# ScalarE issues the stores of what it wrote itself; a first cast and an expert step change their places

## The chip, the cores and the metric

The kernel runs on one core of one Trainium2 chip. Its engines are called PE (TensorE: matmuls, and the loads of their stationary operand as PEld), DVE (VectorE), ACT (ScalarE), POOL (GpSimd) and SP (SyncE, which only issues DMAs here). The metric is the device time of one launch in microseconds (us). The kernel before was run three times: 2190.37 us is the median, from 2181.95 to 2191.92.

## What is computed

The input x has 8 batches of 5696 tokens by 128 channels. Each channel is convolved with a filter h as long as the sequence, and the result goes through a mixture of 8 experts of which each token takes one:

```python
Xf = np.fft.rfft(x, n=2 * S, axis=1)
Hf = np.fft.rfft(h, n=2 * S, axis=0)
y = np.fft.irfft(Xf * Hf[None], n=2 * S, axis=1)[:, :S, :]
...
logits = x @ w_gate                      # x is now y, 45568 x 128
expert_idx = np.argmax(logits, axis=1)
...
for e in range(E):                       # 8 experts
    mask = expert_idx == e
    h = np.maximum(x[mask] @ w1[e], 0.0) # 128 -> 1024
    ye = h @ w2[e]                       # 1024 -> 128
    out[mask] = gate_w[mask, None] * ye
```

## The kernel before

The Fourier transform is split in two steps, both done as matmuls, with the data in device memory between them. The batches form three groups of 2, 3 and 3. Every group goes through three stages:

- **A, forward transform** (`steps_a`). An item is one batch and four of the 48 residues. Its tile xt is loaded (L277), cast to the matmul's type on ACT (L268, tile xc, first half), and the rest that the cast lost is subtracted on POOL or DVE (L269, second half). Both halves go through PE (L290) twice, once for the real part (c = 0) and once for the imaginary part (c = 1). `store` copies the result to the tile ut, the real part on ACT, the imaginary part on DVE (L302). When the last batch of the group is in ut, its store to U is put on the list `late`, and `flush` (L283) issues all on the list from SP, a step later. `start` loads the first items and casts the first one; `begin` loads one item ahead, casts the next one and issues the matmuls.
- **B, products** (`phase_b`). For four frequencies at a time, uq is loaded from U, transformed further (L503 to L509), multiplied with the filter's spectrum hh (L535 to L550), and transformed back (L562, L566). For group 0, `filt` and `filt_save` make the spectrum from h on the way, and a store puts it into HS for the other groups. For groups 1 and 2, ACT copies each result to vt (L587). HS and V (tile vt) also go through a list `late`, which SP works off once per step of the loop (L628).
- **C, inverse and routing** (`phase_c`). vq is loaded from V, cast (L705) and split (L706), transformed (L742), turned, scored against the gate, routed to an expert, ranked among that expert's tokens, and scattered by POOL into SR, which is ordered by expert. The ranks of a part come from counts of earlier tiles: `score` makes two small matmuls with a matrix of ones and a triangular one (L785, L786) on the choices of the tile before, into the tile gb. The last tile's counts are made by `score(None, n - 2)` when nothing is left to score; they need the choices oh of the last tile, which a chain on DVE makes.

Beside B and C of groups 1 and 2 the expert layers run (`experts`): xr is loaded from SR, turned to xtb, multiplied with w1 (L1098, tile mh), the relu is split between ACT (L1104) and DVE (L1108), multiplied with w2 (L1120, tile ma), and written out by POOL (L1143). A step is a quarter of a tile: six matmuls of each layer. The weights wb are loaded by SP from WD (L1067) under a condition, so most of these 728 issues move nothing. C of group g (g = 0, 1) has A of the next group beside it: for group 1 as an ordinary stream (`phase_a`), for group 2 as a **guest** inside C of group 1 (`Guest`, whose `begin` and `end` are called in the loop of `phase_c`). `rest` calls `guest.start()` twelve steps before B of group 1 ends, so that the loads are on their way.

The order is written by hand: all functions are generators, and `run` takes from the stream that has the lowest sum of stated costs so far. What comes out is one fixed list of instructions per engine, and each engine works its list in order. So an instruction that waits holds everything behind it on its engine. `yield STEP` in `phase_c` states a cost without issuing anything, which lets an expert step come first.

DMAs that SP and ACT issue share eight completion counters, taken in turn in the program's order. The DMA that takes a counter waits until the one that had it before, eight places earlier, has landed. Before the change ACT issues only the nine loads of constants (L199) in stage A of group 0; SP issues all other hardware DMAs. POOL has its own queue for the scatters and for one table.

Of the kernel before, what the change touches and what calls it, by code (L numbers as in the profile page):

```python
# [23 lines left out]
NB = 48  # L24
# [35 lines left out]
STEP = 1065  # L60
# [5 lines left out]
def conv_moe(ctx: ExitStack, tc: tile.TileContext, I, out, B, S, D, E, F, split):  # L66
    nc = tc.nc
# [70 lines left out]
    for g, nbs in enumerate(split):  # L138
        gr = Group(g, b0, sum(nbs))
# [9 lines left out]
    HS = dram.tile([NB, QN, 2, D], F32, name="HS")  # L149
# [3 lines left out]
    state = {"rests": False, "hold": 0, "space": False, "spare": None}  # L153
# [97 lines left out]
    def steps_a(gr, tag, bufs):  # L251
        g, nb = gr.g, gr.nb
        srcs = [(I["x"][gr.b0 + b], b) for b in range(nb)]
        tw = 4 * D
        items = []
        for ig in range(NB // 4):
            for src, b in srcs:
                items.append((ig, src, b))
        xts, uts, xss = {}, {}, {}
        fore = 2 if g > 1 else 4  # L260
        split = A3[g]

        def cut(n):
            if not split or n >= len(items):
                return
            xt = xts.pop(n)
            xs = sb.tile([MP, 2, tw], F32R, tag="us", name=f"xc{g}_{n}", bufs=3 if g > 1 else 2)
            nc.scalar.copy(xs[:, 0], xt)  # L268
            getattr(nc, ALO[g]).tensor_tensor(out=xs[:, 1], in0=xt, in1=xs[:, 0].bitcast(F32), op=ALU.subtract)  # L269
            xss[n] = xs  # L270

        def load(n):
            if n >= len(items):
                return
            ig, src, b = items[n]
            xts[n] = sb.tile([MP, tw], F32, tag="xt", name=f"xt{g}_{n}", bufs=1 + fore)
            nc.sync.dma_start(xts[n], src[:, ig * tw : (ig + 1) * tw])  # L277

        banks, late = {}, []

        def flush():
            while late:
                nc.sync.dma_start(*late.pop(0))  # L283

        def transform(m):
            n, c = divmod(m, 2)
            banks[m] = ps.tile([P, 512], F32, tag="cx", name=f"pa{g}_{n}_{c}", bufs=4)
            ops = [(fcs[:, c], xts[n])] if not split else [(fcr[:, u, c], xss[n][:, v]) for u, v in PASSES]
            for k, (lhs, rhs) in enumerate(ops):
                nc.tensor.matmul(banks[m][:QN, :], lhs, rhs, start=(k == 0), stop=(k == len(ops) - 1))  # L290
            if c == 1:
                (xss if split else xts).pop(n)

        def store(m):
            n, c = divmod(m, 2)
            ig, src, b = items[n]
            if b == 0:
                uts[c] = sb.tile([QN, 4, gr.cols], F32, tag=tag, name=f"ut{g}_{ig}_{c}", bufs=bufs)
            srcv = banks.pop(m)[:QN, :].rearrange("p (i d) -> p i d", d=D)
            lo = c * NB + ig * 4  # L300
            cp = nc.scalar.copy if c == 0 else nc.vector.tensor_copy
            cp(uts[c][:, :, b * D : (b + 1) * D], srcv)  # L302
            if b == nb - 1:
                late.append((gr.U[:, lo : lo + 4, :], uts[c]))

        def start():
            for n in range(fore):
                load(n)
            cut(0)

        def begin(m):
            if m % 2 == 0:
                load(m // 2 + fore)
                cut(m // 2 + 1)
            transform(m)

        return start, begin, store, flush, 2 * len(items)
# [107 lines left out]
    def phase_b(gr):  # L425
        g, cb, cw, nch, QB, PK = gr.g, gr.cb, gr.cw, gr.nch, gr.qb, gr.pk
        iw = PK * cw
        lags = BLAGS[PK - 1]
        tiles, outs_ = {}, {}
# [36 lines left out]

        mats, hhs, hbank, cuts, whole = {}, {}, {}, {}, {}
        cutting = F3[g]
        state, banks, late = {}, {}, []

        def filt(qb, k0):
            if g != 0 or qb * QB >= QN:
# [6 lines left out]
        def filt_save(qb, m):  # L479
            if qb not in hbank:  # L480
                return
            hp = hbank[qb]
            if m == 0:
                hhs[qb] = hhbufs[qb % 3]
            hh = hhs[qb]
            c2, k = divmod(m, 2)
            nc.scalar.mul(hh[k * HP : (k + 1) * HP, :, c2, :], hp[c2 * HP : (c2 + 1) * HP], -1.0 if m == 3 else 1.0)
            if m == 3:
                hbank.pop(qb)
                late.append((HS[:, qb * QB : qb * QB + QB], hh[:NB, :QB]))  # L490

        def forward(n):
            q, c = items[n]
# [81 lines left out]
        def save(n):  # L575
            q, c = items[n]
            qb, k0 = divmod(q, QB)
            if g == 0:
                nc.scalar.copy(
                    wide[:, q : q + PK], banks.pop(n)[:, : PK * cb * K2].rearrange("p (q b x) -> p q b x", b=cb, x=K2)  # L580
                )
                if k0 + PK == QB:
                    tiles.pop(qb), hhs.pop(qb), mats.pop(qb)
                return
            if k0 == 0 and c == 0:
                outs_[qb] = sb.tile([K2, QB, gr.cols], F32, tag="six", name=f"vt{g}_{q}", bufs=SIX)
            nc.scalar.copy(  # L587
                outs_[qb][:, k0 : k0 + PK, c * cw : (c + 1) * cw],
                banks.pop(n)[:K2, :iw].rearrange("p (q x) -> p q x", q=PK),
            )  # L590
            if k0 + PK == QB and c == nch - 1:
                late.append((gr.V[qb * QB : qb * QB + QB].rearrange("q p c -> p q c"), outs_.pop(qb)))
                tiles.pop(qb), hhs.pop(qb), mats.pop(qb)

        items = [(q, c) for q in range(0, QN, PK) for c in range(nch)]
# [17 lines left out]
        for n in range(N + lags[3] + 2):  # L613
            qb, at = divmod(n, per)
            for k0 in range(at * PK, (at + 1) * PK):
                if k0 == 1:
                    load_m(qb + (3 if g == 0 else 2))
                if k0 == min(3, per * PK - 1):
                    load(qb + 2)
                if k0 == 0:  # L620
                    filt(qb + 1, QB - 1)
                    if qb:
                        filt_save(qb, 3)
                else:
                    filt(qb + 2, k0 - 1)
                    filt_save(qb + 1, k0 - 1)
            while late:
                nc.sync.dma_start(*late.pop(0))  # L628
            if n < N:
                forward(n)  # L630
                if n % per == per - 1:
                    load_whole(qb + 2)
            cut(n + CUT)
            dp, dc, di, ds_ = lags
            if 0 <= n - di < N:
                inverse(n - di)
            if 0 <= n - dp < N:
                product(n - dp)
            if 0 <= n - dc < N:
                combine(n - dc)  # L640
            if 0 <= n - ds_ < N:
                save(n - ds_)
            yield PK * max(cw * 7 / 2.4 + 200, 2 * cw / 0.96 + 300) if g == 0 else RATE[3 * g - 2] * iw * 8 / 2.4
# [28 lines left out]
    def phase_c(pt, guest=None):  # L672
        gr, g, nb, cb, cw, NI, ns = pt.gr, pt.s, pt.nb, pt.cb, pt.cw, pt.ni, pt.ns
# [204 lines left out]
        for n in range(n_end + 1):  # L878
            for k in range(nsub):
                at = n * nsub + k  # L880
                if k == (1 if n == 0 else 0):
                    load(n + 2)
                if n < nu:
                    synth(n, k)
                if TL <= at < total_sub + TL:
                    tp = ps.tile([P, 512], F32, tag=ytag, name=f"tp{g}_{n}_{k}", bufs=ybuf)
                    turn(*divmod(at - TL, nsub), tp)
                if k == nsub - 1 and n >= 1:
                    score(n - 1, n - 2 if g else None)
                if k == 0 and n >= (n_end if g else 2):  # L890
                    score(None, n - 2)
                lift(at + 2)
                if guest:
                    guest.begin(1 if k == nsub - 1 and n >= 1 else 2)
                yield cost if n < nu else cost / 2
                if guest:
                    guest.end()
                if n < nu:
                    divide(*divmod(at + AHEAD, nsub))
                    settle(n, k)  # L900
                lifted(at + 2)
                if 0 <= at - TL < total_sub:
                    turned(*divmod(at - TL, nsub))
                chains = []
                if g and k == nsub - 1 and 0 <= n - 2 < nu:
                    chains.append(rank(n - 2))
                if k == nsub - 1 and 0 <= n - 1 < nu:
                    chains.append(route(n - 1))
                if k == 0 and n >= (n_end if g else 2):
                    chains.append(rank(n - 2))  # L910
                zipped(*chains)
                if n == n_end:
                    break
# [515 lines left out]
```

## Time and profile before

| | us |
|---|---|
| median of three runs (lowest, highest) | 2190.37 (2181.95, 2191.92) |
| profiled execution | 2188.59 |
| its span, first to last instruction | 2186.7 |
| mean granted clock of PE, share of full speed | 0.974 |
| stage A of group 0 with the filter's transform | 0 to 81 |
| B of group 0 | 81 to 230 |
| C of group 0 with A of group 1 | 230 to 407 |
| B of group 1, then C of group 1 with the guest | 407 to 720, 720 to 960 |
| B of group 2, then C of group 2 | 960 to 1401, 1401 to 1650 |
| a last stretch of filling and sorting, then experts alone | 1650 to 1700, 1700 to 2187 |

The stages' borders are read from the trace and rounded. In a row of a timeline stand the start, the busy time, the engine, the line, the operation with the tiles it writes and reads, the shape, and in brackets the idle time ahead of it on its engine with what released it. In a row of waits stand the waiting line, what it waited for, the sum, the number of waits and the longest. The granted clock is the share of full speed that the power throttle allowed PE.

The 40 slices of the span give the course of things (busy tenths of each engine; the clock that PE was granted; the share of time that the 16 DMA engines were busy):

```profile
PE   9999899799999999988999999999998999999998
PEld 7889676467676888987888888999998999999998
DVE  5688576799898677768888878666666555555554
ACT  6677555234343566644555545565554444444444
POOL 7466265535454277777878777456664344443333
PEclk9999999699999999999999999999999999999999
DMA  8899798899897798977788787466552443343331
```

### The profile page before, as it was taken

What the parts mean: (1) busy time and instruction counts of PE and PEld (TensorE: products, weight loads), DVE (VectorE), ACT (ScalarE), POOL (GpSimd) and SP (SyncE); (2) the same over time, 40 slices, a digit from 0 to 9 for tenths busy, and PEclk for the clock granted to TensorE, in tenths of its full rate; (3) what the DMA queues carried; (4) which work ended last, traced back from release to release, by engine and by line L of the source; (5) the groups of instructions that cost most, each with busy time, mean ns of one, the idle gap of its engine ahead of it and who ended that gap; (6) DMA issues with size and microseconds to landing.
All of it is one profiled execution on the core that took longest, in us unless ns stands there. A gap on an engine that the chain in (4) does not pass through costs nothing. (4 is left out here: it accounts for less than half of the span.)

```text
span 2186.7 us, 46733 instructions
## 1 busy us (share of the span) xinstructions
PE 2091.7 (96%) x14458; PEld 1864.4 (85%) x14458; DVE 1538.1 (70%) x3365; ACT 1118.7 (51%) x2323; POOL 1236.6 (57%) x1215
## 2 busy tenths in 40 slices
PE   9999899799999999988999999999998999999998
PEld 7889676467676888987888888999998999999998
DVE  5688576799898677768888878666666555555554
ACT  6677555234343566644555545565554444444444
POOL 7466265535454277777878777456664344443333
PEclk9999999699999999999999999999999999999999
DMA  8899798899897798977788787466552443343331
GB/s 279 245 278 292 219 276 262 247 230 260 229 256 182 215 278 255 269 197 210 199 223 225 190 210 197 137 163 170 125 139 80 141 129 106 128 130 125 121 119 34
DMA packets 218366, 424.80 MB, mean 194 GB/s; under 512 B 32661, under 2 KB 136587, under 8 KB 218116
## 3 DMA queue, kind: packets, MB, share of 16 engines
q1 hardware_dynamic: 189711, 365.62, 60.6%
q0 software_dynamic: 27296, 55.94, 8.8%
q8 instruction: 117, 1.92, 0.4%
q14 instruction: 133, 1.09, 0.2%
q10 hardware_dynamic: 1109, 0.23, 0.1%
HBM read 582.74 MB, written 154.27 MB: 337 GB/s over the span
## 5 line engine op out<-in xcount | busy, mean ns | idle before, releaser
L1108 DVE SCALAR_TENSOR_TENSOR hs<-mh,hs 128x512 fp32r<-128x512 f32 x728 | 501.7, 689 | 394.7 <-ACT hs L1104 388.1
L1098 PE MATMUL mh<-xtb,wb 128*128 128x256 f32 x4368 | 703.5, 297 | 22.9 <-DMA wb<-WD 17.8
L1104 ACT ACTIVATE hs<-mh 128x512 fp32r<-128x512 f32 x728 | 435.8, 599 | 482.2 <-PE mh L1098 478.2
L1120 PE MATMUL ma<-hs,wb 128*128 128x256 f32 x4368 | 659.3, 287 | 11.1 <-DMA wb<-WD 11.1
L1098 PEld LDWEIGHTS mh<-xtb,wb 128*128 128x128 f32 x4368 | 590.8, 191 | 92.8 <-issue 38.6
L1120 PEld LDWEIGHTS ma<-hs,wb 128*128 128x128 f32 x4368 | 574.6, 191 | 14.1 <-DMA wb<-WD 13.7
L1143 POOL DMA_INDIRECT out<-xr x314 | 311.6, 992 | 438.5 <-DVE xr L1134 372.6
L655 POOL DMA_INDIRECT SR<-rt,pi x384 | 408.4, 1064 | 242.2 <-issue 74.9
L550 POOL TENSOR_TENSOR zt<-zt,xs 128x384 f32<-128x384 f32 (+1 forms) x280 | 297.2, 1070 | 138.7 <-DVE xs L540 84.4
L587 ACT COPY vt<-vp 96x384 f32<-96x384 f32 x240 | 114.3, 476 | 270.3 <-PE vp L566 268.5
L544 DVE TENSOR_TENSOR xs<-xp,hh 64x384 f32<-64x384 f32 (+1 forms) x360 | 214.8, 597 | 7.8
L535 DVE TENSOR_TENSOR zt<-xp,hh 128x384 f32<-128x384 f32 (+1 forms) x300 | 173.6, 579 | 40.6 <-PE xp L509 27.4
L566 PE MATMUL vp<-zt,mi 128*96 128x384 f32 x480 | 201.4, 501 | 0.3 <-issue 0.3
L509 PE MATMUL xp<-uq,mt 96*128 96x256 f32 (+1 forms) x480 | 172.1, 464 | 9.6 <-ACT vt L587 5.6
L290 PE MATMUL pa<-xc,fcr 120*120 120x512 f32 x576 | 163.8, 417 | 7.2 <-ACT hh L727 5.4
L540 DVE SCALAR_TENSOR_TENSOR xs<-xp,hh 64x384 f32<-64x384 f32 x240 | 134.3, 560 | 4.2
L290 PEld LDWEIGHTS pa<-xc,fcr 120*120 120x120 f32 x576 | 99.5, 187 | 34.3 <-ACT hh L727 8.0
L742 PE MATMUL yp<-vr,gcr 120*120 120x384 f32 x576 | 119.2, 342 | 7.3 <-ACT ut L302 5.8
L566 PEld LDWEIGHTS vp<-zt,mi 128*96 128x96 f32 x480 | 79.3, 167 | 49.9 <-issue 27.6
L509 PEld LDWEIGHTS xp<-uq,mt 96*128 96x128 f32 x480 | 86.1, 203 | 34.8 <-ACT vt L587 13.0
L706 DVE TENSOR_TENSOR vr<-vq,vr 120x768 fp32r<-120x768 f32 x96 | 91.5, 954 | 30.8 <-ACT vr L705 30.2
L742 PEld LDWEIGHTS yp<-vr,gcr 120*120 120x120 f32 x576 | 97.4, 185 | 10.5 <-ACT ut L302 8.1
(160 smaller groups left out, 2572.1 us busy)
## 6 DMA issues: line engine op xcount, KB each, us to landing
wb<-WD SPq DMA_DIRECT2D x728, 512.0 KB
U<-ut SPq DMA_DIRECT2D x48, 720.0 KB
uq<-U SPq DMA_DIRECT2D x60, 576.0 KB
V<-vt SPq DMA_DIRECT2D x60, 576.0 KB
vq<-V SPq DMA_DIRECT2D x48, 720.0 KB
xt<-x SPq DMA_DIRECT2D x96, 240.0 KB
hh<-HS SPq DMA_DIRECT2D x120, 192.0 KB
xr<-SR SPq DMA_DIRECT2D x157, 130.0 KB
```

Of the source, the lines that this page charges most:

```text
L290: nc.tensor.matmul(banks[m][:QN, :], lhs, rhs, start=(k == 0), stop=(k == len(ops) - 1))
L509: nc.tensor.matmul(to, mt[:, k0 + s, :], uc, start=True, stop=True)
L544: nc.vector.tensor_tensor(out=xs[to], in0=x3[at], in1=him, op=ALU.mult)
L550: eng.tensor_tensor(out=zt, in0=zt, in1=xs, op=ALU.add)
L566: nc.tensor.matmul(vp[:K2, s * cw : (s + 1) * cw], mi[:, k0 + s, :], zt[:, s].rearrange("p b d -> p (b d)"), start=True, stop=True,)
L655: s = nc.gpsimd.indirect_dma_start(out=SR[:, :], out_offset=IndirectOffsetOnAxis(ap=pi[:, b : b + 1], axis=0), in_=rt[:, b, :], in_offset= ...
L742: nc.tensor.matmul(yp[:MP, :cw], lhs, rhs, start=(m == 0), stop=(m == len(ops) - 1))
L1098: nc.tensor.matmul(hp[:, u, :], wb[:, a, f, :], xt[:, b, :], start=(n == 0), stop=(n == 2))
L1104: done = nc.scalar.activation(hs[:, 0], hp, AF.Relu)
L1108: nc.vector.scalar_tensor_tensor(out=hs[:, 1], in0=hp, scalar=0.0, in1=hs[:, 0].bitcast(F32), op0=ALU.max, op1=ALU.subtract)
L1120: nc.tensor.matmul(accs[j], wb[:, a, f, :], hs[:, b, u, :], start=(k == 0 and u == 0 and n == 0), stop=(k == NPAIR - 1 and u == 1 and n == 2),
L1143: sc = nc.gpsimd.indirect_dma_start(out=out[:, :], out_offset=IndirectOffsetOnAxis(ap=xr[:, s, D + 1 : D + 2].bitcast(I32), axis=0), in_=x ...
```

## The change

Three things are edited.

1. **Stores.** The store of U's real half, of HS and of V is issued by ACT (`nc.scalar.dma_start`), right behind ACT's own copy, in place of the list that SP works off. U's imaginary half, which DVE writes, stays on the list and on SP. These are 36 + 30 + 60 = 126 issues, and the loop over the list in `phase_b` goes.
2. **First cast.** `cut(0)` moves from `start` to `begin(0)`. For `phase_a` the two follow each other, and nothing moves. For the guest, `start` comes during B of group 1 and `begin(0)` in C of group 1.
3. **Counts.** Ahead of the last `score(None, n - 2)` of parts 1 and 2 stands a `yield STEP`.

```diff
@@ store, in steps_a
             if b == nb - 1:
-                late.append((gr.U[:, lo : lo + 4, :], uts[c]))
+                if c == 0:
+                    nc.scalar.dma_start(gr.U[:, lo : lo + 4, :], uts[c])
+                else:
+                    late.append((gr.U[:, lo : lo + 4, :], uts[c]))
 
         def start():
             for n in range(fore):
                 load(n)
-            cut(0)
 
         def begin(m):
+            if m == 0:
+                cut(0)
             if m % 2 == 0:
@@ phase_b
-        state, banks, late = {}, {}, []
+        state, banks = {}, {}
...
-                late.append((HS[:, qb * QB : qb * QB + QB], hh[:NB, :QB]))
+                nc.scalar.dma_start(HS[:, qb * QB : qb * QB + QB], hh[:NB, :QB])
...
-                late.append((gr.V[qb * QB : qb * QB + QB].rearrange("q p c -> p q c"), outs_.pop(qb)))
+                nc.scalar.dma_start(gr.V[qb * QB : qb * QB + QB].rearrange("q p c -> p q c"), outs_.pop(qb))
...
-            while late:
-                nc.sync.dma_start(*late.pop(0))
             if n < N:
@@ phase_c
                 if k == 0 and n >= (n_end if g else 2):
+                    if g:
+                        yield STEP
                     score(None, n - 2)
```

The following rows are the instructions of one engine in their order, with the line, the operation, and the tiles written and read; the numbers at the end of a name tell buffers apart and differ between the two kernels. Lines of the changed kernel lie up to four further down. First ACT during B of group 1, before the change, where the guest's first cast (xc_0) stands between copies to vt, which PE's next results need out of their way:

```order
L1088 CAST xtb_7941<-mx_16_7900 128x256
L587 COPY vt_100_7925<-vp_102_0_7929 96x384
L1104 ACTIVATE hs_3_7981<-mh_3_7951 128x512
L587 COPY vt_100_7925<-vp_103_0_7972 96x384
L268 CAST xc_0_8025<-xt_0_8021 120x512
L587 COPY vt_104_8041<-vp_104_0_8012 96x384
L1104 ACTIVATE hs_0_8043<-mh_0_7997 128x512
```

Then ACT in the changed kernel at the beginning of C of group 1, where it stands now:

```order
L1108 ACTIVATE hs_0_8645<-mh_0_8632 128x512
L707 CAST vr_0_0_8663<-vq_0_8528 120x768
L707 CAST vr_0_1_8666<-vq_0_8528 120x768
L268 CAST xc_0_8676<-xt_0_8022 120x512
L268 CAST xc_1_8681<-xt_1_8024 120x512
L1108 ACTIVATE hs_1_8692<-mh_1_8648 128x512
```

The cast went from between two groups of four copies to behind the casts of vr, right ahead of item 1's cast; DVE's subtraction L269 went with it.

Next SP at the end of B of group 1, before the change: the last store of V among the loads of weights (each has an ISA row that reads its condition).

```order
L1067 ISA
L1067 DMA wb_0_0_4784<-WD 128x1024
L1067 ISA
L1067 DMA wb_0_3_4790<-WD 128x1024
L628 DMA V_73<-vt_116_8406 96x4x384
L1067 ISA
L1067 DMA wb_0_1_4786<-WD 128x1024
```

And ACT in the changed kernel, with the same store:

```order
L1134 COPY ot_8447<-ma_8294 128x256
L591 COPY vt_116_8403<-vp_118_0_8421 96x384
L591 COPY vt_116_8403<-vp_119_0_8468 96x384
L596 DMA V_73<-vt_116_8403 96x4x384
L1108 ACTIVATE hs_2_8473<-mh_2_8449 128x512
L1092 CAST xtb_8476<-mx_19_8456 128x256
```

The store left SP's row and stands on ACT directly behind the copy that completes vt, ahead of a relu.

Last PE at the end of C of group 2, where the last counts (gb_None) are made, before the change:

```order
L791 MATMUL gb_23_22_24349<-c_moe_w_gate,yt_23_24292 120x8 x6
L785 LDWEIGHTS ones
L785 MATMUL gb_None_24382<-oh_23_24376,ones 128x54
L786 LDWEIGHTS lt
L786 MATMUL gb_None_24382<-oh_23_24376,lt 120x54
L1098 MATMUL mh_0_24403<-xtb_24328,wb_0_0_13345 128x256 x6
L1120 MATMUL ma_24284<-hs_2_24322,wb_0_3_13518 128x256 x6
```

And in the changed kernel:

```order
L793 MATMUL gb_23_22_24349<-c_moe_w_gate,yt_23_24292 120x8 x6
L1102 MATMUL mh_0_24400<-xtb_24328,wb_0_0_13345 128x256 x6
L1124 MATMUL ma_24284<-hs_2_24322,wb_0_3_13518 128x256 x6
L787 LDWEIGHTS ones
L787 MATMUL gb_None_24413<-oh_23_24376,ones 128x54
L788 LDWEIGHTS lt
L788 MATMUL gb_None_24413<-oh_23_24376,lt 120x54
```

One expert step (mh, ma) went ahead of the two count matmuls; at the end of C of group 1 the same happens.

## The prediction

> **What bounds the kernel now.** I read the page's table of engines first, then the table by stage, then the waits of PE, and last the waits of the queues. The first line gives busy time, share of the span and number of instructions of each engine.
>
> ```profile
> PE 2091.7 (96%) x14458; PEld 1864.4 (85%) x14458; DVE 1538.1 (70%) x3365; ACT 1118.7 (51%) x2323; POOL 1236.6 (57%) x1215
> ```
>
> PE is the bound: of the span of 2186.7 us only 95.0 us (2186.7 less 2091.7) are idle on PE. A change that takes no matmul away can win only from these 95 us and from stretches at a lower granted clock. ACT, which gets the new work, is idle for half of the span. The table by stage gives for each stretch its length, the busy time of PE, PEld, DVE, ACT and POOL, the granted clock, the DMA share and GB/s.
>
> ```profile
> 81.00:230.00 149.00, 138.97 (x955) 129.57 (x956) 124.58 (x183) 104.33 (x195) 95.38 (x76) 0.97 0.99 270
> 230.00:407.00 177.00, 161.55 (x861) 120.58 (x859) 112.90 (x338) 90.42 (x201) 90.82 (x85) 0.97 0.85 252
> 407.00:720.00 313.00, 297.55 (x1475) 209.95 (x1476) 274.90 (x529) 110.24 (x236) 153.11 (x155) 0.91 0.90 232
> ```
>
> The rows are the products of the first group, its inverse with the next group's forward transform beside it, and the products of the second group. They hold 41 of the 95 us (10.0 + 15.5 + 15.5), at a DMA share of 0.85 to 0.99. The experts alone, which come last, hold none of the edits and stay. PE's waits (us in total, times, longest) over the whole span:
>
> ```profile
> PE mh L1098 <- DMA wb<-WD: 17.8, 11, 3.3
> PE ma L1120 <- DMA wb<-WD: 11.1, 8, 3.2
> PE gb_None L785 <- DVE sm L826: 7.9, 11, 1.6
> PE yp L742 <- ACT ut L302: 5.8, 5, 1.9
> PE xp L509 <- ACT vt L587: 5.6, 7, 2.2
> PE pa L290 <- ACT hh L727: 5.4, 6, 1.3
> PE xp L509 <- DMA uq<-U: 4.0, 2, 3.1
> ...
> PE ph L390 <- ACT uc L405: 1.6, 2, 0.9
> ```
>
> Nothing here is one big wait. Loads of weights (17.8 and 11.1) are the largest, and all go through SP's queue. That queue waits in order; its own rows are:
>
> ```profile
> SPq L283 <- ACT ut L302: 65.7, 26, 7.7
> ...
> SPq L628 <- ACT vt L587: 28.4, 21, 5.5
> ...
> SPq L443 <- DMA uq<-U: 20.6, 12, 2.6
> ...
> SPq L628 <- ACT hh L487: 10.5, 13, 3.8
> ```
>
> So SP stands 104.6 us (65.7 + 28.4 + 10.5) ahead of stores whose data ACT has not written yet, with later loads behind them. These three waits go. What remains of SP's limits is in the third row: it waits for landings, because each DMA takes one of eight counters in turn and can't issue before the DMA eight places earlier has landed.
>
> **The guest's first cast.** The ACT row (start, length, in brackets the idle time before it and its releaser), PE's row, and the table of stretches around them:
>
> ```profile
> 681.38 0.62 ACT L268 CAST xc<-xt 120x512 fp32r<-120x512 f32 x1 [6.05 <-DMA xt<-x]
> ```
>
> ```profile
> 682.43 1.65 PE L509 MATMUL xp<-uq,mt 96*128 96x384 f32 x2 [2.17 <-ACT vt L587]
> ```
>
> ```profile
> 640.00:680.20 40.20, 39.77 (x218) 29.31 (x215) 34.26 (x64) 14.14 (x30) 21.84 (x23) 1.00 1.01 267
> 680.20:682.40 2.20, 0.06 (x1) 0.00 (x0) 0.37 (x1) 1.02 (x3) 0.00 (x0) 0.98 1.01 306
> 682.40:689.10 6.70, 6.67 (x21) 4.91 (x22) 6.53 (x12) 2.07 (x5) 2.00 (x2) 0.50 0.90 225
> ```
>
> ACT waits 6.05 us for a load that nobody needs for another 50 us; the V copies behind it are late, PE stands for 2.17 us, and then the granted clock is 0.50 for 6.7 us. In that stretch PE did 21 matmuls in 6.70 us, 3.13 per us, where ahead of the gap it did 218 in 40.20, 5.42 per us. So it did 3.9 us worth of work (6.70 x 3.13 / 5.42) and lost 2.8. Together 2.17 + 2.8 = 5.0 us, an estimate, since the matmuls differ in size; if only half of 6.7 is lost it is 5.5. What is late next? DVE, with 6.53 of 6.70 busy: but it is catching up there after the same stall, and ahead of it ran at 34.26 of 40.20. The cast's new place is here, in ACT, DVE and PE rows:
>
> ```profile
> 730.67 0.62 ACT L268 CAST xc<-xt 120x512 fp32r<-120x512 f32 x1
> ```
>
> ```profile
> 731.81 0.69 DVE L269 TENSOR_TENSOR xc<-xt,xc 120x512 fp32r<-120x512 f32 x1
> ```
>
> ```profile
> 732.99 1.56 PE L290 MATMUL pa<-xc,fcr 120*120 120x512 f32 x6
> ```
>
> These are item 1's cast, its subtraction, and item 0's matmul. With the change item 0's cast takes the slot at 730.67 and its subtraction ends at 732.50, still ahead of 732.99; item 1 comes 0.6 to 0.7 us later and has until its own matmuls. The cost lies between 0 and 1.3 us (0.62 + 0.69); I take 0, because PE is at that time in the inverse's matmuls. **-5.0.**
>
> **Stores on ACT: what SP gains.** Of one place all rows are seen: SP's row of V and of the weights behind it, then PE's wait, then the clock.
>
> ```profile
> 716.43 0.32 SPq L628 DMA_DIRECT2D V<-vt  x1
> 717.11 1.83 SPq L1067 DMA_DIRECT2D wb<-WD  x2
> ```
>
> ```profile
> 722.90 1.29 PE L1098 MATMUL mh<-xtb,wb 128*128 128x256 f32 x6 [1.88 <-DMA wb<-WD]
> ```
>
> ```profile
> 723.30:726.70 3.40, 3.40 (x18) 3.40 (x17) 1.38 (x3) 0.97 (x2) 0.18 (x1) 0.50 1.03 275
> ```
>
> Without the store the weights could issue up to 0.68 us earlier (717.11 less 716.43), more only if their own buffer were free before. The bounds are 0 and 3.6 (the wait of 1.88 and half of 3.40 at half clock); I take 1.5, since one part of the clock's loss may go with the shorter gap. All other places together, among them one where a store of V stands ahead of weights and the rest where no store does, I put at 0.5; the bound above is the sum of the load rows, in the first rival. In the first transform the last real halves of U stand in SP behind loads for the next stage, and PE's row of L390 shows what that costs: 1.6 us, so 0 to 1.6, and I take 0.8. The imaginary halves stay on SP and hold it at the same places as now. **-2.8.**
>
> **Stores on ACT: what ACT pays.** 126 issues move: 36 of U, 30 of HS, 60 of V. No store has ever been issued on ACT here; the nearest rows are those on SP (min/median/max ns).
>
> ```profile
> L283 SPq DMA_DIRECT2D U<-ut x72: 316/328/2895, 10.7 to 951.8; - x72
> ```
>
> ```profile
> L628 SPq DMA_DIRECT2D V<-vt x60: 317/334/1459, 436.5 to 1394.2; - x60
> L628 SPq DMA_DIRECT2D HS<-hh x30: 308/376/1105, 84.4 to 220.6; - x30
> ```
>
> By the medians that is 36 x 0.328 + 30 x 0.376 + 60 x 0.334 = 43.1 us more on an engine that is idle for 1068 us. Each store also waits for the copy right ahead of it on ACT, so it hides behind nothing on ACT itself; it is hidden where ACT's next instruction waits for PE anyway. For V (60) and U of the last group (12) that holds, since the relu behind them is what waits for PE:
>
> ```profile
> ACT hs L1104 <- PE mh L1098: 478.2, 566, 5.0
> ```
>
> I take 0, between 0 and 2. In the stages without experts cover is thin. The first is the spectrum's store in the first group's products:
>
> ```profile
> 103.93 0.59 ACT L487 ACTIVATE hh<-hp 64x512 f32<-64x512 f32 x1 [0.59 <-ACT hh L487]
> ```
>
> ACT has a pause of 0.59 us, the shorter kind, where the store now stands, and 0.376 fits. If each issue took the row's maximum of 1.1, 0.5 would stick out, 15 us over 30 stores; I take the median and +1. In the first transform 12 stores are 3.9 us, with ACT waiting for PE between (+1, from 0 to 4). In the first inverse 12 more are 3.9 us, and there PE already waits for ACT's copies (L727 5.4, in the list above), so half shows: +2, from 0 to 4. **+4, between 0 and 25.**
>
> **The counts.** PE's rows at the end of groups 1 and 2, and the next waits after the first of them:
>
> ```profile
> 959.98 0.20 PE L785 MATMUL gb_None<-oh,ones 120*128 120x54 bf16 x1 [1.65 <-DVE sm L826]
> ```
>
> ```profile
> 967.71 0.94 PE L1098 MATMUL mh<-xtb,wb 128*128 128x256 f32 x6 [1.25 <-DMA wb<-WD]
> ```
>
> ```profile
> 1649.46 0.18 PE L785 MATMUL gb_None<-oh,ones 120*128 120x54 bf16 x1 [1.64 <-DVE sm L826]
> ```
>
> Six matmuls of layer 1 take 0.94 us (the second row), and a step moves six of each layer into each gap of 1.65. The first gain is lost: 8 us later PE waits for weights that stand in SP behind loads bound to U's last landing, and comes there sooner only to wait longer. The second has a stretch behind it that SP's loads partly hold too; I keep most of it: **-1.5**, between 0 and 3.3. The step's own DMAs are not issued sooner, for its tokens were loaded steps before; SP's dummy stores of the fill that follows shift by one step.
>
> **The sum.** -5.0 - 2.8 + 4.0 - 1.5 = -5.3 us. The profiled execution took 2188.59 us, 1.9 over its span; the runs' median is 2190.37, between 2181.95 and 2191.92, so the profiled one is a typical run. 2188.59 - 5.3 = 2183.3, so **2183 us**. About 0.5% (11 us) is what a measurement of this kernel can tell from no change, so the likeliest reading is the same, on the fast side; its own range is 2176 to 2192.
>
> **Rivals.** *SP's freedom is worth more (0.30).* If the loads come earlier all through, a third of 32.9 us (17.8 + 11.1 + 4.0 of PE's list) goes, 11 us, and one more half-clock stretch like that at 682.4, about 3. With the cast's 5.0, the counts' 1.5, the first transform's 0.8 and ACT's +4 that is -17 us: 2171. For it: 104.6 us of SP's waiting. Against it: DMA share is 0.90 to 0.99 in these stages, so a load issued earlier shares the same engines with the same stores; and the eight counters let SP go at most eight DMAs past a store that has not landed. The Trainium skill, "DMA: Bandwidth & Descriptors", section "Issuing engines are not separate DMA queues", speaks against it as well: whichever engine starts a DMA, it runs on the same 16 engines, and only the sequencer's time to initiate is saved. By that rule the stores' part would be nothing but SP's issue time, and the sum -3.3 in place of -5.3.
>
> *ACT's issues lengthen the lead stages: slower (0.14).* The place is the stage from 81 to 230 us, DMA share 0.99, and the two transforms around it. The price is that of a long issue: rows reach 1.1 (HS) and 2.9 us (U). The gains above are 9.3, so a time over 0.5% slower needs 20 us of issue that shows, 0.16 us for each of 126 stores; with the 15 us of HS and 4 + 4 for U, the sum is 23 - 9.3 = +14: 2202. For it: ACT's own copy must end before each issue, and the next copy stands behind. Against it: SP's long rows stand right behind other large issues, and on ACT the stores stand alone. By the Trainium skill, "Perfetto Trace Analysis", section "DMA Instruction — HWDGE (DVE, Sync)", a reported issue includes a wait for a descriptor generator that sequencers share; no row here shows two queues competing for it.
>
> *The change doesn't do what it says (part of "same").* SP still stops at U's imaginary halves and eight DMAs past each store, and the cast's 5 us are taken back by the weights at 717 us, where PE waits for loads that are bound to SP: -5.3 + 5.0 + 2.0 = +1.7, 2190.
>
> **How the numbers follow.** The forecast with the last rival has 0.56, the first 0.30, the second 0.14. The range goes from 2167, past the first rival, to 2197, which leaves out most of the second and the far end of the first. Faster by over 0.5%: 0.29; within: 0.58; slower: 0.13.
>
> **What would show it.** Right: no gap near 680 us on PE, and clock 1.00 behind it; SP's rows for L283 and ACT, and for L628, gone; issues of U, V and HS on ACT's queue at about 0.35 us; L785's wait down from 7.9 by some 3; the experts alone as long as before. Wrong: ACT issues of 1 us or more; new waits of PE for ACT in the first 407 us; load waits (17.8 and 11.1) that halve or grow; a gap at 722 us that has taken up what was won at 680.

## The result: slower, and the profile after

The changed kernel takes 2212.57 us (median of four runs, 2211.01 to 2225.77) against 2188.97. The ratio is 1.0133, 95% interval 1.0107 to 1.0158: 1.3% slower, about 29 us by the ratio (the two medians lie 23.6 us apart), where the forecast was 5 us faster than before. The profiled execution took 2211.01 us, its span is 2209.2. First the page's row of engines:

```profile
PE 2090.2 (95%) x14458; PEld 1859.4 (84%) x14458; DVE 1537.7 (70%) x3365; ACT 1118.5 (51%) x2323; POOL 1231.2 (56%) x1215
```

PE's work is unchanged. Its idle time went from 95.0 to 119.0 us (2209.2 less 2090.2), so the loss is all waiting. Who is waited for stands in PE's list (us in total, times, longest), here its first two rows and that of the counts, and in SP's:

```profile
PE mh L1102 <- DMA wb<-WD: 19.9, 14, 3.9
PE ma L1124 <- DMA wb<-WD: 17.0, 10, 3.6
...
PE gb_None L787 <- DVE sm L828: 4.6, 9, 1.4
```

```profile
SPq L283 <- DVE ut L302: 130.2, 29, 13.1
...
SPq L1071 <- DMA V<-vt: 16.9, 8, 7.9
SPq L1045 <- DMA V<-vt: 16.3, 7, 3.3
SPq L461 <- DMA V<-vt: 15.5, 10, 3.4
...
SPq L464 <- DMA HS<-hh: 12.4, 7, 3.1
...
SPq L447 <- DMA V<-vt: 6.3, 2, 4.2
```

The waits for ACT at SP's stores are gone, as the change says. In their place SP waits for *landings* of V and HS, at loads that have nothing to do with them: weights (L1071), tokens (L1045), uq (L461), matrices (L447, L464). PE's waits for weights grew from 28.9 to 36.9 us. Over all of PE's rows, waits for DMAs grew from 36.5 to 51.6 us, and waits for ACT from 30.2 to 37.5 us; what ACT itself waited for there was not followed up. U's wait did not go: SP now stands at the imaginary half for 130.2 us, where it stood 110.5 (65.7 + 44.8) at both halves.

ACT's issues themselves are as short as hoped (min/median/max ns):

```profile
L596 ACTq DMA_DIRECT2D V<-vt x60: 311/312/358, 439.4 to 1421.8; - x60
```

One place shows the mechanism. ACT's copy and store, then SP's row of four weight loads and the tokens' loads behind, then SP's wait in that window, then PE:

```profile
438.88 0.47 ACT L591 COPY vt<-vp 96x384 f32<-96x384 f32 x1 [3.02 <-PE vp L570]
439.38 0.33 ACTq L596 DMA_DIRECT2D V<-vt  x1
```

```profile
438.18 9.87 SPq L1071 DMA_DIRECT2D wb<-WD  x4
449.12 2.60 SPq L1045 DMA_DIRECT2D xr<-SR  x3
```

```profile
SPq L1071 <- DMA V<-vt: 7.9, 1, 7.9
```

```profile
452.27 0.69 PE L174 MATMUL mxNone<-ident,xr 128*128 128x128 f32 x2 [2.95 <-DMA xr<-SR]
```

SP had issued three weight loads by 439.7. The fourth takes the counter of the V store eight places earlier in the program, which ACT issued at 439.38 and which landed 8.3 us later; the load went out at 447.71. The tokens behind it came late, and PE stood for 2.95 us. The places, worked out from the trace and the program's order:

```
place in the program   engine  start    landed   waits for the counter of
368  V<-vt             ACT     439.38   447.69   360
375  wb<-WD            SP      439.31   446.22   367
376  wb<-WD            SP      447.71   451.25   368 (V<-vt), landed 447.69
377  xr<-SR            SP      449.12   452.22   369
```

Over the whole trace, SP's list has 32 such waits for a landing of V, 69.1 us in all (the loads of V itself, L689, left out), and 9 for HS, 17.6 us. Before, SP's waits at the same stores (L628 from 403 to 1405 us, its two largest rows) were these:

```profile
SPq L628 <- ACT vt L587: 28.4, 21, 5.5
SPq L628 <- DMA uq<-U: 11.6, 10, 2.3
```

That is 40.0 us, and 5.3 us more stand in that list as waits of other loads for a landing of V (L464, L443, L450). At the store SP needed the copy's end, and for 11.6 us the counter of a load of uq; now a load needs the landing of the store, 5.9 us from issue on the mean.

Two steps of the forecast hold in the same trace. Near 680 us of before (692 here) PE has no gap and runs at full speed, and the offset between the two executions at the same matmul (the later start in the changed kernel counts as plus) falls there by 5.5 us. The stretch, with its length, the busy time of PE, PEld, DVE, ACT and POOL, the granted clock, the DMA share and GB/s:

```profile
685.00:699.00 14.00, 14.00 (x78) 10.35 (x77) 13.12 (x25) 5.36 (x12) 7.91 (x8) 1.00 0.78 213
```

At the last counts and the fill the offset falls by 3.7 us more (from +26.2 to +22.6). One more jump taught something about the baseline: at 579 us the profiled execution of before has a gap of 2.20 us with a half clock behind it, which the changed kernel's trace and five others (e0 to e4) do not have: their offset falls there by 5 to 7 us, of which up to 5.5 come back at the next loads. It belonged to that one execution:

```profile
578.83 0.97 PE L1098 MATMUL mh<-xtb,wb 128*128 128x256 f32 x6 [2.20 <-DMA wb<-WD]
```

### The profile page after: what moved, and what is told of

Its sections match the earlier page's. It is cut to its first block, busy times and chain, and to the rows that moved or that the text cites. A ratio compares the mean times of both kernels' runs of the same rounds, so it can differ in the third digit from the quotient of the medians.

```text
span 2209.2 us, 46668 instructions
## 1 busy us (share of the span) xinstructions
PE 2090.2 (95%) x14458; PEld 1859.4 (84%) x14458; DVE 1537.7 (70%) x3365; ACT 1118.5 (51%) x2323; POOL 1231.2 (56%) x1215
## 4 chain that ended last, share of the span: by engine, by line
PE 65%; DMA 10%; issue 4%; DVE 2%; POOL 1%; SPq 1%; ACT 1%; POOLq 0%; DVEq 0%; ACTq 0%
PE ma L1124 20%; PE mh L1102 20%; PE vp L570 6%; PE yp L744 4%; DMA wb<-WD 4%; PE xp L513 3%; PE mx L174 3%; PE gb L793 2%; PE pa L290 2%; DMA uq<-U 2%; PE xp L507 2%; DMA xt<-x 2%; PE tp L174 1%; POOL out L1147 1%; PE xp L511 1%
## 5 line engine op out<-in xcount | busy, mean ns | idle before, releaser
L1102 PE MATMUL mh<-xtb,wb 128*128 128x256 f32 x4368 | 703.8, 297 | 27.2 <-DMA wb<-WD 19.9
L554 POOL TENSOR_TENSOR zt<-zt,xs 128x384 f32<-128x384 f32 (+1 forms) x280 | 296.2, 1068 | 142.9 <-DVE xs L544 40.0
```

The costliest lines, as they stand in the source:

```text
L554: eng.tensor_tensor(out=zt, in0=zt, in1=xs, op=ALU.add)
L1102: nc.tensor.matmul(hp[:, u, :], wb[:, a, f, :], xt[:, b, :], start=(n == 0), stop=(n == 2))
```

## The experiments

Theory A: ACT's stores share eight completion counters with SP's loads, and SP waits for their landing. Theory B: ACT's time for the issue costs. Theory C: a second queue's traffic slows SP's loads. Theory D: SP running further ahead is bad in itself. Every ratio is against the kernel before in the same runs. Runs e0, e5 to e7 and e12 to e17 came on chips on which the kernel before takes 2274 to 2295 us, and there only ratios are compared.

### The parts alone

Each edit of the change is put alone into the kernel before (e1 holds the cast and the counts):

```diff
+            if m == 0:                       # e1, in begin, and not in start
+                cut(0)
+                    if g:                    # e1, ahead of score(None, n - 2)
+                        yield STEP
+                if c == 0:                   # e2
+                    nc.scalar.dma_start(gr.U[:, lo : lo + 4, :], uts[c])
+                nc.scalar.dma_start(gr.V[...], outs_.pop(qb))      # e3
+                nc.scalar.dma_start(HS[...], hh[:NB, :QB])         # e4
```

> The kernel before with the guest's first cast and the step ahead of the last counts moved, all stores on SP. Theory A (the stores on ACT cost all, through the eight shared counters) and B (ACT's issue time) and C (traffic of a second queue) all expect a gain here: about -5.5 us for the cast (the gap of 2.2 us near 680 us and the half clock behind it go) and 0 to -3 us for the counts, so 2180 to 2184 against 2189. The rival that the cast or the step is what costs expects +3 us or more.

> Only U's real half on ACT. Theory A: 12 stores in each of three stages; few loads stand eight places behind, so +2 to +6 us, with SP waiting for landings of U. Theory B: the price is paid in the two transforms without experts, +3 to +8 us, with new waits of PE for ACT there. Theory C: near 0, since the bytes are the same.

> Only V on ACT. Theory A: the largest part, +8 to +16 us, SP waiting some 60 us for landings of V that ACT issued, where it waited 41 us (28.4 for the copies, 12.7 for a counter) at the stores before, and PE's waits for wb and xr grow. Theory B: within 2 us, since the relu behind the store waits for PE anyway. Theory C: loads (wb, uq) land later by 0.5 us or more from issue.

> Only HS on ACT. Theory A: +3 to +6 us between 81 and 230 us, SP waiting some 16 us for landings of HS, and PE's wait hp<-mt growing from 3.6 to about 7. Theory B: +1 to +10 us in the same stage, but as waits of PE for hh on ACT. Theory C: 0 to 1 us.

| run | ratio | 95% interval | us by the ratio |
|---|---|---|---|
| e1 cast and counts | 0.9966 | 0.9942 to 0.9991 | -7.4 |
| e2 U on ACT | 1.0040 | 1.0017 to 1.0063 | +8.7 |
| e3 V on ACT | 1.0113 | 1.0080 to 1.0147 | +24.7 |
| e4 HS on ACT | 1.0013 | 0.9988 to 1.0038 | +2.8 |

The sum is 28.8 us, and the change as a whole gave 29; but each part's interval is 5 to 7 us wide either way. V is nearly all of it, twice what I expected of it alone. U cost more than any theory expected, and theory A does not explain it: in the trace of e2 SP's loads were held for 4.1 us by landings of U that ACT had issued. Theory C expected loads that land later. From issue to landing, on the mean over all that moved data, the traces of before and after give:

```
            before   after
wb<-WD      5.88     5.61
uq<-U       6.71     6.19
V<-vt       4.91     5.91
```

The loads land sooner, so C falls for them; they are issued later. HS alone is within noise, though SP's waits for its landings are there (13.5 and 8.4 us in its list), and PE's wait for the matrices mt at hp grew from 3.6 to 9.9 us.

### ACT's time without a DMA

```diff
+    scr = const.tile([P, 160], F32, name="scr")
...
+                if c == 0:
+                    nc.scalar.copy(scr[:QN, :160], uts[c][:, 3, gr.cols - 160 :])
+                nc.scalar.copy(scr[HP : HP + NB, :D], hh[HP : HP + NB, QB - 1, 1, :])
+                nc.scalar.copy(scr[:K2, :160], outs_[qb][:, QB - 1, gr.cols - 160 :])
```

> The kernel before, all stores on SP, and on ACT behind each copy that completes U's real half, HS or V a small copy of 128 to 160 elements per partition from the tile just written into a scratch tile: 126 instructions of ACT time of about the length of an issue, with no DMA. The result is the reference's. Theory A: within 5 us of the kernel before. Theory B (ACT's time is what costs): +15 us or more, of them the larger part in the stages before 407 us.

> The run with 126 more small copies on ACT and all stores on SP once more, if it comes on a chip where the kernel before takes 2185 to 2190. Theory A: within 5 us of the kernel before. Theory B: +15 us or more.

> The 126 small copies on ACT, stores on SP, for the third time, since both runs so far came on a chip where the kernel before takes 2274 to 2278. If this one comes on a chip of 2185 to 2190: theory A within 5 us of the kernel before, theory B +15 us or more.

```profile
L596 ACT COPY scr<-vt x60: 324/326/329, 437.6 to 1445.2; 96x160 f32<-96x160 f32 x60
L307 ACT COPY scr<-ut x36: 325/326/338, 11.4 to 996.5; 120x160 f32<-120x160 f32 x36
```

The added copies last as long as the issues (326 ns against 312). Ratios: 0.9968 (0.9947 to 0.9990), 0.9969 (0.9943 to 0.9996) and 0.9970 (0.9944 to 0.9996). So B falls on these chips: 126 such pieces of ACT time cost nothing. That they make the kernel 0.3% faster no theory expected, and I have no explanation. None of the three came on the faster chips, where V's 24.7 us were measured.

### V on a queue with counters of its own

```diff
-                late.append((gr.V[...], outs_.pop(qb)))
+                nc.gpsimd.dma_start(gr.V[...], outs_.pop(qb))
```

> The kernel before with V's 60 stores issued by GpSimd, whose DMAs have completion counters of their own; so the store leaves SP's queue, is a transfer of another queue, and costs ACT nothing. Theory A (counters): SP no longer waits for landings of V, so nothing like the +24 us of V on ACT: within 8 us of the kernel before, either way, since GpSimd now waits for the copies of ACT in its own order. Theory C (traffic of a second queue beside SP's loads) and theory D (SP runs ahead and its far loads get in front of urgent ones): +15 us or more, as on ACT. Theory B: no gain and no loss.

> The kernel before once more, for a second trace: which of its gaps (72, 87, 579 us) are in every execution and which in one alone. All theories expect the same time, 2182 to 2192.

e5 gave 1.0063 (1.0039 to 1.0087), 14 us slower: what C and D expected, and A not. The traces of e5 and e0 (the kernel before on the same chip) split it: the products of group 1, from the first to the last of PE's xp matmuls, took 288.0 us against 294.7, those of group 2 took 401.2 against 386.7. A trace's figure for group 1 scatters, though: e6, e15 and e16, which are one program, have 293.9, 294.3 and 286.7 us. In group 2 these three lie between 384.0 and 384.7, so the 14.5 us there are clear of it. In that stretch of e5 SP stood 13.6 us at the tokens' loads for landings of uq (2.1 in e0), and PE 16.4 us for weights (7.3 in e0). So group 1 does not speak against A, and in group 2 C, D or GpSimd's time for the issues may be the cause; which of them was not tested. The next runs therefore take group 1 alone, with the cast and the counts moved in all four (as in e1), so that only the issuing engine of V differs:

```diff
+                if g == 1:                                          # e8; e9: scalar; e10: scalar, g == 2
+                    nc.gpsimd.dma_start(gr.V[...], outs_.pop(qb))
...
+                if g == 1:                                          # e11 = e8 and this
+                    nc.scalar.dma_start(tiny[0:1, 16 * qb : 16 * qb + 16], outs_[qb][0:1, QB - 1, gr.cols - 16 :])
```

> The kernel with the cast and the counts moved and all stores on SP, and of these the 30 stores of V of group 1 on GpSimd. Theory A (an ACT store holds SP through the shared counters until it has landed; without the counters it would not): the products of group 1 (403 to 723 us before) get shorter by some 5 to 9 us, as in the run with all V on GpSimd (-8.7 there), and the whole 10 to 16 us faster than the kernel before. Theory D (SP running ahead is bad in itself) and C (a second queue's traffic is): longer than with V on SP, by 8 us or more.

> The same with these 30 stores on ACT in place of GpSimd. Theory A: 15 to 20 us slower than on GpSimd, SP waiting over 40 us in that stage for landings of V. Theories C and D: the same as on GpSimd within 5 us. Against the kernel before: A +3 to +8.

> The 30 stores of V of group 2 on ACT, those of group 1 on SP, cast and counts moved. With V on ACT in both groups at +24.7 (cast and counts not moved) and group 1 at +11.7 by its trace, A expects +10 to +14 for group 2, less 7.4 for cast and counts: +3 to +7 against the kernel before.

> V of group 1 on GpSimd as in e8, and besides one DMA of 64 bytes from ACT behind each of these 30 stores' last copy, into a scratch tensor: it takes a turn of the shared counters from ACT, but no bandwidth. Theory A: SP waits for landings of these tiny DMAs eight places on, and a good part of what GpSimd won in the products of group 1 is lost: 3 to 12 us slower than e8 (less than V on ACT, since 64 bytes land sooner than 576 KB). Theories B, C and D: within 2 us of e8.

| run | V of group 1 | V of group 2 | ratio | 95% interval | products of group 1, us |
|---|---|---|---|---|---|
| e1 | SP | SP | 0.9966 | 0.9942 to 0.9991 | 290.4 |
| e8 | GpSimd | SP | 0.9964 | 0.9944 to 0.9983 | 285.0 |
| e9 | ACT | SP | 1.0023 | 0.9998 to 1.0048 | 299.2 |
| e10 | SP | ACT | 1.0003 | 0.9981 to 1.0025 | 286.3 |
| e11 | GpSimd, and 64 bytes by ACT | SP | 0.9991 | 0.9974 to 1.0009 | 293.8 |

The same 30 stores cost 13 us more on ACT than on GpSimd (1.0023 less 0.9964, of 2185; the means of the two kernels' own fast runs, all on one chip, differ by 11.2 us), with the same bytes on a queue other than SP's and SP free of the store in both. C and D expected no difference; A does, though 15 to 20. e11 is the test of the counters: 30 DMAs of 64 bytes carry no traffic worth the name, and still the whole grows by 0.0027, 6 us. The two intervals against the kernel before overlap a little, but the twelve runs of e11 against the twelve of e8, on the same chip, differ by 5.6 us on the mean, with a 95% interval of 2.8 to 8.5. The stage grows from 285.0 to 293.8 us, little more than such a figure scatters between traces of one program. SP's list of e11 says where it was held:

```profile
SPq L445 <- DMA tiny<-vt: 13.6, 8, 3.0
SPq L1076 <- DMA tiny<-vt: 3.7, 1, 3.7
SPq L1050 <- DMA tiny<-vt: 3.5, 4, 1.3
```

Loads of matrices, weights and tokens wait until 64 bytes of ACT's have landed, 3.7 us from issue on the mean. These 30 issues also take 0.22 us of ACT each, which by the copies above costs nothing (on the slower chips). With V itself on ACT (e9) the same kind of row is larger, over five lines 52.8 us, of which two:

```profile
SPq L1047 <- DMA V<-vt: 13.3, 5, 3.7
...
SPq L461 <- DMA V<-vt: 12.0, 4, 7.5
```

e8 did not bring the 10 to 16 us expected of it: against e1 (on another chip of the same speed) it is the same. GpSimd takes V off SP, but what it wins in this stage (285.0 against 290.4 and, with SP too, 286.3) is not more than the traces scatter. In group 2, V on ACT costs 8 us (e10 less e1), where 10 to 14 were expected. The trace of e10 does not show where: the products of group 2 took 391.5 us there against 392.4 in e1, and SP's loads were held for 10.5 us by ACT's stores. So the counters are shown as the cause in group 1, which has some 12 of V's 24.7 us (e9 less e1); for group 2 the list of the changed kernel shows the same kind of wait, and what it costs there is not shown by itself.

### The change without V, and U in parts

```diff
-                nc.scalar.dma_start(gr.V[...], outs_.pop(qb))       # e7, e17: the changed kernel, with the list again
+                late.append((gr.V[...], outs_.pop(qb)))
...
-                if c == 0:
+                if c == 0 and g == 0:                               # e12; e13: g > 0
                     nc.scalar.dma_start(gr.U[:, lo : lo + 4, :], uts[c])
...
+                if c == 0:                                          # e14, U on SP
+                    nc.scalar.dma_start(tiny[0:1, 16 * (QN * g + ig) :][:, :16], uts[c][0:1, 3, gr.cols - 16 :])
```

> The changed kernel with V's stores back on SP; U's real half and HS stay on ACT, the cast and the counts stay moved. If the parts add up: -7.4 (cast and counts) + 8.7 (U) + 2.8 (HS) = +4 us against the kernel before, so V alone makes the change slow. If the parts act on one another, it stays at +15 us or more.

> The changed kernel with V back on SP once more, for the same reason. If the parts measured alone on the faster chip add up there: +4 us (from -6 to +14); as on the slower chip: -4 us. At +15 or more the parts act on one another.

> Only the 12 stores of U's real half of group 0 on ACT (first transform, 0 to 81 us). If U's +8.7 us are half of it there, as the stage's end in the traces says (88.3 us in the two runs with U on ACT, 84.4 on the mean of eight without): +3 to +5 us. Theory A: by waits for landings; theory B: by ACT's time beside the copies.

> Only the 24 stores of U's real half of groups 1 and 2 on ACT. By the same traces +2 us in the inverse of group 0 and the rest in the inverse of group 1: +3 to +6 us. If neither this nor e12 costs anything, the +8.7 was noise (its interval begins at 3.7).

> U on SP as before, and one DMA of 64 bytes from ACT behind each of the 36 copies that complete U's real half: ACT's issue time and turns of the counters, without moving a store. Theory A: up to +4 us, less than U itself, since 64 bytes land sooner. Theory B: the same +8.7 as U on ACT. Neither: 0.

Without V's stores the change is no slower than before: 0.9983 (0.9961 to 1.0005) and again 0.9981 (0.9954 to 1.0009), on the slower chips, inside what the parts' sum allows. U stays open. Group 0 alone gave 1.0021 (0.9998 to 1.0045), groups 1 and 2 gave 0.9986 (0.9960 to 1.0011), the tiny DMAs 1.0000 (0.9977 to 1.0022): groups 0 to 2 together 0.0007, under 2 us, where U as a whole had given +8.7 on the faster chip. Whether U costs less on the slower chips, or the first value lay high, these runs do not settle.

## Why the prediction was wrong

- **What bounds the kernel:** right. PE's work stayed the same, and the 24 us came as idle time, 15 of them in waits for DMAs.
- **The guest's first cast, -5.0:** right. The gap and the half clock are gone, worth 5.5 us in the changed kernel's trace; with the counts, e1 gives -7.4.
- **The counts, -1.5:** right in direction, too small. The first place gave nothing, as said; the second and the fill gave 3.7 us in the changed trace, and some 3 in e1's.
- **What ACT pays, +4:** wrong, and with it the second rival, which had the right side and nearly the size (2202) by a mechanism that is not there. Issues took 0.31 to 0.32 us, and the same time on ACT without a DMA cost nothing (e6, e15, e16, on the slower chips). That its 2202 lies near the result is luck.
- **What SP gains, -2.8: here the prediction failed.** It took the three rows of SP's waits (104.6 us) as waits that go, and the eight counters as something that only limits the gain ("eight DMAs past a store that has not landed"). It priced ACT's issues by their length, but did not ask what SP's loads would wait for behind ACT's stores. A store that SP issued itself held SP until the copy ended, and the eighth DMA behind it found it landed or nearly (5.3 us of such waits for V). A store on ACT holds SP at the eighth place until ACT has reached it, *and* until it has landed. Of the DMAs that use up the eight places many are weight loads that move nothing (600 of 728), so SP gets there fast. For V the held time rose from 45.3 us (40.0 and 5.3) to 69.1 us, and V alone costs 24.7 us. One sign that the prediction named for being wrong came true: the load waits of 17.8 and 11.1 us grew, to 19.9 and 17.0.
- **The third rival** named this limit, and priced it at no gain (2190) where it is a loss. Its term was bounded at zero on the wrong side: the 20.6 us that SP waited for landings of uq (L443) stood in the prediction's own rows, to show that such waits are not free.
- **The first rival** (SP's freedom is worth more): not so. Its argument of a DMA share of 0.90 to 0.99 left out the 0.85 of the stage from 230 to 407 us, without harm. Even with V off SP and off the shared counters (e8) the kernel is no faster than with V on SP (e1). The rule that it cited from the Trainium skill, "DMA: Bandwidth & Descriptors", section "Issuing engines are not separate DMA queues" (what moving an issue saves is the sequencer's time), agrees as far as it goes: there was no gain. That rule names no loss, and the loss that e9 and e11 show is not in the transfers but in the order of their completions.
- **The likeliest case and the range:** the range ended at 2197 because the slower case was given 0.14 and one mechanism. The stage from 81 to 230 us, where it put the price, took 143.5 us from first to last xp matmul against 138.0, but 143.7 in e8 too, where HS is on SP. Most came later: in the products of group 2 the changed kernel's offset grows from +16.3 to +27.9 us. In the products of group 1 the two traces take nearly the same time (296.2 us against 296.8), because the one of before holds the cast's gap and the gap at 579 us there; with the cast in its old place everywhere, e3 (V on ACT) took 309.0, and e2 and e4 (V on SP) 295.3 and 290.6.

Of the kernels tried, the one with only the cast and the counts moved (e1, 0.9966) and the one that has V of group 1 on GpSimd besides (e8, 0.9964) are faster than both kernels of this case.

## What to carry to other kernels

A DMA moved to another engine takes its completion counter with it: where queues share counters in turn, list for each moved DMA what stands one turn behind it in the other queue, and price that at the landing, not at the issue. Test it with a DMA of a few bytes in the same place: if that alone costs time, traffic is not the cause; an instruction as long as the issue, without a DMA, tests the engine's time. And a gap in one profiled execution is not yet a gap of the kernel: hold a second trace against it before a term of the sum rests on it.

## What the runs showed of the hardware

The kernel before took 2185 to 2189 us on some chips and 2274 to 2295 us on others. Between the two traces of it (span 2186.7 and 2283.0) the largest difference lies in the inverse of group 1, from the first to the last of PE's yp matmuls 221.3 against 273.5 us, at a granted clock of 0.97 against 0.87, with longer pauses of ACT and DVE behind PE and of PE behind ACT; its cause was not sought. On the slower chips 126 copies of 0.3 us added to ACT made the kernel 0.3% faster, three times.
